# A fused attention and feed-forward kernel: third-weight loads moved ahead of a batch, and that batch's phases moved later among the weight products

## The chip, the cores and the metric

One Trainium2 chip, one core. The metric is device time in microseconds (us) from launch to end, as the median of several executions. The profile's "span" is the part of one execution from its first to its last instruction.

## What is computed

The reference is sparse attention with 8 batches, 8 heads, 576 tokens and 64 channels a head. Heads 0 to 3 look back over the last 31 tokens and themselves (local), heads 4 to 7 over tokens at multiples of 32 (strided). The attended values, as 4608 tokens of 512 channels, go through a multiplicative feed-forward layer:

```python
mask_local = (rel >= 0) & (rel < stride)
mask_strided = (rel >= 0) & (pos[None, :] % stride == pos[:, None] % stride)
...
attn = attn / (np.sum(attn, axis=-1, keepdims=True) + 1e-09)
return np.matmul(attn, v).astype(np.float32)
...
a = x @ w1
b = x @ w2
h = a * b @ w3
return (h @ w_out).astype(np.float32)
```

q, k and v are [8, 8, 576, 64], w1 and w2 [512, 1024], w3 [1024, 1024], w_out [1024, 512], all float32. The kernel works in float16 with float32 accumulation.

## The kernel before

**Folding.** Since nothing stands between the last two products, w3 @ w_out is computed once in the kernel (`w34`, [1024, 512]). w3 comes in 8 blocks of 128 rows (`load_w3`, L149). `fold_tr(jc)` (L528) transposes block jc on TensorE (PE), eight 128x128 transposes into one PSUM bank, then DVE copies one half of it into `w3T[0]` and ACT the other into `w3T[1]`. `fold_mm(jc)` (L537) multiplies by w_out in two halves of four products each, and DVE (even jc) or ACT (odd jc) copies the result to `w34`.

**Loads.** Every load is a DMA issued by SP, in the order in which the code calls it, into one of nine float32 staging buffers; a cast on GpSimd (POOL), in the same order, makes the float16 copy. For a batch: `load_qk(b, 0)` and `load_qk(b, 1)` bring the first 512 tokens of q and k for the local and the strided heads, `load_rest(b)` the last 64 tokens of all heads, `load_vL(b)` and `load_vS(b)` the values. A DMA also waits until the earlier transfer that used its semaphore, one of eight, has landed. The output writes, issued by ACT, use the same eight.

**Pairs.** The heads of a batch are worked in four pairs, two local and two strided; `pairs[4:8]` (p4 to p7) are batch 1, p8 is the first of batch 2. The first two batches go phase by phase: `ah_T` (L321) transposes q and k of a pair, `ah_R` (L343) the last 64 tokens of all pairs of the batch, `ah_S` (L395) makes the scores in two halves, with an exponential on ACT and a mask product on DVE (L403) for each, `ah_PV(s, g)` (L407) multiplies one half by the values and normalizes on DVE (`norm`, L422, two instructions, L426 and L427), `ph_T2` (L430) transposes the result into `xT` (ACT copies). From batch 2 on `ph_TS(s, t)` (L557) makes the scores of pair s and the transposes of pair t together, `ph_PV` (L300) the values product (PE at L317); `ph_TS(None, p8)` makes p8's transposes alone, the batch's last 64 tokens among them (PE at L232 and L240).

**Tiles.** The feed-forward part goes over 9 tiles of 512 tokens: `ab_parts(tch)` (L447) gives 32 steps of two products each, four steps for one block of 128 columns (a over channels 0 and 1, a over channels 2 and 3, b likewise), `o_parts(tch)` (L496) 16 steps of the output product, with an ACT copy and a DMA write to memory for every 128 tokens.

**PSUM.** Three pools: `psF` with three banks (fold, tiles, strided `ah_T`), `psB` with two buffers of two banks (scores, transposes of `ph_TS`, values products), `psM` with one bank (local `ah_T`, `ah_R`, `ph_T2`). A new tile waits until the one that held its buffer has been read.

**Order.** PE's order is the order of the code. The stretch that the change touches is written by hand: `units` holds the 23 fold steps and 8 pairs of output steps of tile 0, and `plan` says after which unit each phase of batch 1 is put:

```python
for jc in range(KF):
    h0, h1 = fold_mm(jc)
    units.append(h0)
    if jc + 1 < KF:
        units.append(lambda jc=jc: fold_tr(jc + 1))
    units.append(h1)
units += halves(o_parts(0))
```

After it, each tile's 48 steps fill the gaps of the list `stream`, which holds the later batches' phases with 48 marks (`GAP`) in a batch; `host(units, upto)` (L631) spreads units evenly over the marks up to `upto`. SP's and POOL's order is the order of the calls; ACT and DVE instructions are put in order by the scheduler of the language.

Of the kernel before, what the change touches and what calls it, by code (L numbers as in the profile page):

```python
# [19 lines left out]
def kernel(  # L20
# [49 lines left out]
    def pe(ins):  # L70
        return tc.keep_in_program_order(ins)

    def copy(eng, out, in_):
        if eng == "a":
            nc.scalar.copy(out=out, in_=in_)  # L75
        elif eng == "v":
            nc.vector.tensor_copy(out=out, in_=in_)  # L77
        else:
            nc.gpsimd.tensor_copy(out=out, in_=in_)  # L79
# [63 lines left out]
    def load_wo(g, eng):  # L143
        src = moe_w_out.rearrange("(c p) n -> p c n", p=P)
        st = stgp.tile([P, 2, DM], FP32, tag="stg")
        nc.sync.dma_start(st, src[:, 2 * g:2 * g + 2, :])
        copy(eng, woh[:, 2 * g:2 * g + 2, :], st)

    def load_w3(jc, eng):  # L149
        st = stgp.tile([P, DF], FP32, tag="stg")  # L150
        nc.sync.dma_start(st, moe_w3[bass.ds(jc * P, P), :])
        t = ffn.tile([P, DF], FP16, tag="w3n", bufs=6)
        w3n[jc] = t
        copy(eng, t, st)
# [13 lines left out]
    def load_qk(b, grp, engs="pp"):  # L168
        for nm, ten, eng in (("q", q, engs[0]), ("k", k, engs[1])):
            st = stgp.tile([P, 4, 4, D], FP32, tag="stg")  # L170
            nc.sync.dma_start(st.rearrange("p h c d -> p h (c d)"),  # L171
                              ten[b, 4 * grp:4 * grp + 4, 0:NM].rearrange("h (p c) d -> p h (c d)", c=4))
            t = qkp.tile([P, 4, 4, D], FP16, tag=f"{nm}{grp}")
            copy(eng, t, st.rearrange("p h c d -> p c h d"))
            x16[(b, nm, grp)] = t

    def load_rest(b, eng="p"):
        st = stgp.tile([P, H, D], FP32, tag="stg")
        for i, ten in enumerate((q, k)):
            nc.sync.dma_start(st[64 * i:64 * i + 64], ten[b, :, NM:S].rearrange("h p d -> p h d"))  # L180
        t = qkp.tile([P, H, D], FP16, tag="r")
        copy(eng, t, st)
        x16[(b, "r")] = t
# [246 lines left out]
    def ph_T2(s):  # L430
        w, n = s.w, s.n
        ps = psM.tile([P, 1024], FP16, tag="m")
        for t in range(n):
            pe(nc.tensor.transpose(ps[:, t * w:(t + 1) * w],  # L434
                                   s.xqs[0:w, t].rearrange("p h d -> p (h d)"),
                                   id16[0:w, 0:w]))
        o = xT[s.hp][:, S * s.b:S * s.b + S]
        if s.local:
            copy("a" if s.b < AHEAD else "v", o, ps[:, 0:S])
        else:  # L440
            nc.scalar.copy(out=o.rearrange("x (p c) -> x p c", c=n),  # L441
                           in_=ps[:, 0:S].rearrange("x (c p) -> x p c", p=w))
# [4 lines left out]
    def ab_parts(tch):  # L447
        tok = bass.ds(tch * NT, NT)
        res = []

        def first():
            abts[tch] = ffn.tile([P, KF, NT], FP16, tag="abt", bufs=4, name=f"abt{tch}")

        for jc in range(KF):
            st = {}

            def a(qt, jc=jc, st=st):
                if qt == 0:
                    if jc == 0:
                        first()  # L460
                    st["a"] = psF.tile([P, NT], FP32, tag="f", name="aps")
                for ci in (2 * qt, 2 * qt + 1):
                    pe(nc.tensor.matmul(st["a"], w1h[:, ci, bass.ds(jc * P, P)], xT[ci][:, tok],  # L463
                                        start=(ci == 0), stop=(ci == KM - 1)))
                if qt:
                    asb = ffn.tile([P, NT], FP32, tag="asb")
                    nc.scalar.copy(out=asb, in_=st["a"])  # L467
                    st["asb"] = asb

            def bb(qt, jc=jc, st=st):  # L470
                if qt == 0:
                    st["b"] = psF.tile([P, NT], FP32, tag="f", name="bps")
                for ci in (2 * qt, 2 * qt + 1):
                    pe(nc.tensor.matmul(st["b"], w2h[:, ci, bass.ds(jc * P, P)], xT[ci][:, tok],  # L474
                                        start=(ci == 0), stop=(ci == KM - 1)))
                if qt:
                    nc.vector.tensor_mul(abts[tch][:, jc, :], st["b"], st["asb"])  # L477

            res += [lambda f=f, qt=qt: f(qt) for f in (a, bb) for qt in range(2)]
        return res  # L480

    def acc_parts(lhs, rhs, done, n):
        st = {}
        m = KF // n

        def part(i):
            if i == 0:
                st["ps"] = psF.tile([P, NT], FP32, tag="f", name="ops")
            for ci in range(m * i, m * i + m):
                pe(nc.tensor.matmul(st["ps"], lhs(ci), rhs(ci), start=(ci == 0), stop=(ci == KF - 1)))  # L490
            if i == n - 1:
                done(st["ps"])

        return [lambda i=i: part(i) for i in range(n)]

    def o_parts(tch):  # L496
        res = []
        for ts in range(NT // P):
            def done(ps, ts=ts):
                osb = ffn.tile([P, DM], FP32, tag="osb", bufs=3)  # L500
                nc.scalar.copy(out=osb, in_=ps)  # L501
                nc.scalar.dma_start(out_r[tch * (NT // P) + ts], osb)

            if tch + 1 < NTILE or ts + 1 < NT // P:
                res += acc_parts(lambda ci, ts=ts: abts[tch][:, ci, bass.ds(ts * P, P)],
                                 lambda ci: w34[:, ci, :], done, 4)
        return res
# [38 lines left out]
    stream = []  # L546
    batch_end = {}
# [68 lines left out]
    for p, s in enumerate(pairs):  # L616
        b, i = divmod(p, 4)
# [11 lines left out]
    pos = [0]  # L629

    def host(units, upto):  # L631
        n = len(units)
        total = sum(x is GAP for x in stream[pos[0]:upto])
        done = 0
        for i, u in enumerate(units):
            tgt = total * i // n
            while pos[0] < upto and (stream[pos[0]] is not GAP or done < tgt):
                x = stream[pos[0]]
                pos[0] += 1
                if x is GAP:  # L640
                    done += 1
                else:
                    x()
            u()
        for x in stream[pos[0]:upto]:
            if x is not GAP:
                x()
        pos[0] = upto
# [9 lines left out]
    load_w3(0, "p")  # L658
    for g in range(4):
        load_wo(g, "p")  # L660
    load_w3(1, "p")
    load_w3(2, "p")
    load_qk(1, 0)
    load_w3(3, "p")
    load_rest(1)
    load_w3(4, "p")
    load_vL(1, (0,))
    load_w3(5, "p")
    load_w3(6, "p")
    load_vL(1, (1,))  # L670
    load_w3(7, "p")
    load_qk(1, 1)
    load_vS(1)

# [10 lines left out]
    units = []  # L685
# [4 lines that stand above are left out]
# [1 line left out]
        units.append(h1)  # L691
    units += halves(o_parts(0))
    p4, p5, p6, p7, p8 = pairs[4:9]
    plan = ((6, ah_T, p4), (9, ah_R, 1), (10, ah_T, p5), (11, ah_S, p4), (13, ah_S, p5),
            (14, ah_PV, p4, 0), (15, ah_PV, p4, 1), (18, ph_T2, p4), (20, ah_PV, p5, 0), (21, ah_PV, p5, 1),
            (21, ah_T, p6), (22, ah_T, p7), (23, ph_T2, p5), (23, ah_S, p6), (24, ah_S, p7),
            (26, ah_PV, p6, 0), (27, ah_PV, p6, 1), (27, ph_TS, None, p8), (28, ah_PV, p7, 0),
            (29, ph_T2, p6), (29, ah_PV, p7, 1), (31, ph_T2, p7))
    for i, u in enumerate(units, 1):
        u()  # L700
        if i == 23:
            load_qk(2, 1)
            load_vS(2)
        for x in plan:
            if x[0] == i:
                x[1](*x[2:])
    for tch in range(1, NTILE):
        units = ab_parts(tch) + o_parts(tch)
        if tch + 1 < B:
            more = tch + 2 < B  # L710
            if more:
                load_qk(tch + 2, 0)
                load_rest(tch + 2)
                load_vL(tch + 2)
            marks = [i for i in range(pos[0], batch_end[tch + 1]) if stream[i] is GAP]
            mid = marks[len(marks) // 2 - 1] + 1
            host(units[0:24], mid)
            if more:
                load_qk(tch + 2, 1)
                load_vS(tch + 2)  # L720
            host(units[24:], batch_end[tch + 1])
        else:
            for u in units:
                u()
# [31 lines left out]
```

## Time and profile before

| | |
|---|---|
| median of 3 runs | 279.38 us (278.61 to 280.46) |
| the profiled execution | 279.19 us |
| its span | 277.5 us |
| PE busy | 261.1 us (94%) |
| DVE, ACT, POOL busy | 145.7, 147.6, 116.1 us |
| read and written | 38.80 and 9.44 MB |

"Busy" counts the time in which an engine has at least one instruction at work. Matmuls overlap one another, so a step's cost on PE is the distance between the starts of its matmuls, not the sum of their durations. In a timeline row the columns are start, duration from the first start to the last end, engine, line, operation, output and inputs, count, and in brackets the idle time before it and who ended it. In a windows row they are the stretch, its length, then busy time and instructions of PE, PE's weight loads, DVE, ACT and POOL, the granted clock, the mean busy share of the 16 DMA engines (transfers that overlap can push it over 1) and GB/s.

### The profile page before, as it was taken

What the parts mean: (1) busy time and instruction counts of PE and PEld (TensorE: products, weight loads), DVE (VectorE), ACT (ScalarE), POOL (GpSimd) and SP (SyncE); (2) the same over time, 40 slices, a digit from 0 to 9 for tenths busy, and PEclk for the clock granted to TensorE, in tenths of its full rate; (3) what the DMA queues carried; (4) which work ended last, traced back from release to release, by engine and by line L of the source; (5) the groups of instructions that cost most, each with busy time, mean ns of one, the idle gap of its engine ahead of it and who ended that gap; (6) DMA issues with size and microseconds to landing.
All of it is one profiled execution on the core that took longest, in us unless ns stands there. A gap on an engine that the chain in (4) does not pass through costs nothing.

```text
span 277.5 us, 6652 instructions
## 1 busy us (share of the span) xinstructions
PE 261.1 (94%) x2656; PEld 138.2 (50%) x2656; DVE 145.7 (53%) x281; ACT 147.6 (53%) x298; POOL 116.1 (42%) x134
## 2 busy tenths in 40 slices
PE   1889998788999999999999999999999999999995
PEld 0465454454555555555555555555555555444442
DVE  2565341745477547655765567466547653320320
ACT  2663335657666566656556564656665654323322
POOL 4677774965856947785585644100000000000000
PEclk9999999999999999999999999999999999999999
DMA  7999999999899989997999680210031012003004
GB/s 208 274 333 391 393 324 258 287 212 147 258 300 223 259 246 266 235 258 192 261 267 240 183 224 4 98 56 2 0 117 40 0 40 113 0 2 151 0 4 151
DMA packets 56752, 48.68 MB, mean 175 GB/s; under 512 B 29200, under 2 KB 45840, under 8 KB 56720
## 3 DMA queue, kind: packets, MB, share of 16 engines
q1 hardware_dynamic: 51536, 38.87, 55.8%
q10 hardware_dynamic: 5184, 9.37, 9.1%
q8 instruction: 21, 0.34, 0.5%
q14 instruction: 11, 0.09, 0.1%
HBM read 38.80 MB, written 9.44 MB: 174 GB/s over the span
## 4 chain that ended last, share of the span: by engine, by line
PE 75%; DMA 14%; POOL 4%; SPq 3%; DVE 1%; issue 1%; ACT 1%; POOLq 0%; ACTq 0%
PE ops L490 21%; PE aps L463 21%; PE bps L474 20%; DMA st<-in_moe_w_dram 8%; DMA st<-in_v_dram 6%; PE sps L317 4%; PE ps L434 3%; POOL t L79 2%; PE pt L232 2%; PE sps L275 2%; PE pt L275 1%; POOL v16L L193 1%; SPq L191 1%; DVE ptm L403 1%; SPq L171 1%
## 5 line engine op out<-in xcount | busy, mean ns | idle before, releaser
L474 PE MATMUL bps<-xT,w2h 128*128 128x512 f16 x288 | 76.1, 379 | 0.0
L463 PE MATMUL aps<-xT,w1h 128*128 128x512 f16 x288 | 74.6, 380 | 0.5 <-ACT xT L441 0.5
L477 DVE TENSOR_TENSOR abt<-bps,asb 128x512 f16<-128x512 f32 x72 | 49.4, 687 | 43.3 <-PE bps L474 28.1
L467 ACT COPY asb<-aps 128x512 f32<-128x512 f32 x72 | 43.1, 599 | 46.3 <-PE aps L463 44.7
L490 PE MATMUL ops<-w,abt 128*128 128x512 f16 x280 | 66.8, 379 | 0.0
L79 POOL CAST t<-st 128x1024 f16<-128x1024 f32 (+1 forms) x46 | 45.7, 1004 | 24.4 <-DMA st<-in_k_dram 11.9
L463 PEld LDWEIGHTS <-w1h 128*128 128x128 f16 x288 | 26.4, 98 | 29.7
L474 PEld LDWEIGHTS <-w2h 128*128 128x128 f16 x288 | 26.3, 98 | 27.6 <-POOL w2h L79 0.8
L490 PEld LDWEIGHTS <-abt 128*128 128x128 f16 x280 | 25.3, 98 | 26.5
L193 POOL CAST v16L<-st 32x768 f16<-32x768 f32 (+1 forms) x32 | 27.7, 865 | 14.3 <-DMA st<-in_v_dram 7.9
L501 ACT COPY osb<-ops 128x512 f32<-128x512 f32 x35 | 20.6, 588 | 19.4 <-PE ops L490 19.4
L295 ACT ACTIVATE pte<-sps 128x960 f16<-128x960 f32 (+1 forms) x24 | 23.9, 995 | 10.8 <-PE sps L275 10.8
L427 DVE TENSOR_TENSOR xqs<-sps,rcp 96x768 f16<-96x768 f32 (+1 forms) x24 | 24.4, 1018 | 0.5
L204 POOL CAST v16S<-st 72x1024 f16<-72x1024 f32 x16 | 17.1, 1074 | 17.4 <-PE pm L317 9.9
L296 DVE TENSOR_TENSOR ptm<-pte,maskL 128x1152 f16<-128x1152 f16 x12 | 11.5, 961 | 22.7 <-ACT pte L295 22.7
L441 ACT COPY xT<-ps 128x576 f16<-128x576 f16 x16 | 10.2, 640 | 22.7 <-PE ps L434 22.7
L296 DVE TENSOR_TENSOR ptm<-pte,maskS 72x1152 f16<-72x1152 f16 x12 | 10.4, 864 | 20.2 <-ACT pte L295 20.2
L75 ACT COPY qT<-pt 128x256 f16<-128x256 f16 (+2 forms) x48 | 17.6, 409 | 3.6 <-DVE kT L77 2.9
L317 PEld LDWEIGHTS <-ptm 72*128 72x128 f16 (+1 forms) x336 | 13.1, 97 | 6.5 <-DVE ptm L296 2.0
L490 PE MATMUL ops<-woh,w3T 128*128 128x512 f16 x64 | 16.1, 379 | 0.0
L434 PEld LDWEIGHTS <-xqs 72*128 72x128 f16 (+1 forms) x224 | 12.1, 97 | 7.5 <-DVE xqs L427 0.8
L434 PE MATMUL ps<-id,xqs 72*128 72x72 f16 (+1 forms) x224 | 13.5, 200 | 0.3 <-DVE xqs L427 0.3
(93 smaller groups left out, 252.2 us busy)
## 6 DMA issues: line engine op xcount, KB each, us to landing
out_dram<-osb ACTq DMA_DIRECT2D x35, 256.0 KB, 2.0
st<-in_q_dram SPq DMA_DIRECT2D x16, 512.0 KB, 5.7
st<-in_k_dram SPq DMA_DIRECT2D x16, 512.0 KB, 4.7
st<-in_moe_w_dram SPq DMA_DIRECT2D x16, 512.0 KB, 10.6
st<-in_v_dram SPq DMA_DIRECT2D x32, 144.0 KB, 6.1
st<-in_v_dram SPq DMA_DIRECT2D x16, 256.0 KB, 7.8
st<-in_moe_w_out_dram SPq DMA_DIRECT2D x4, 512.0 KB
st<-in_q_dram SPq DMA_DIRECT2D x8, 128.0 KB, 7.8
```

Source lines behind the costliest of these rows:

```text
L79: nc.gpsimd.tensor_copy(out=out, in_=in_)
L193: nc.gpsimd.tensor_copy(out=vt[pr, hs, :, 0:D], in_=st[pr])
L295: nc.scalar.activation(out=pte[0:kr, lo:hi], in_=src, func=AF.Exp, bias=0.0, scale=scale)
L296: nc.vector.tensor_mul(ptm[0:kr, 0:2 * S].rearrange("p (a x) -> p a x", x=w), pte[0:kr].rearrange("p (a x) -> p a x", x=w), _ap(mk, 0, [[m ...
L317: pe(nc.tensor.matmul(xps[:, h, i * 65:i * 65 + 65], s.ptm[0:kr, c0:c0 + P], vt[0:kr, 2 * (s.hp % 2) + h, c, :], start=True, stop=True))
L427: nc.vector.tensor_mul(s.xqs[0:w, c0:c0 + l].rearrange("p i h d -> p h i d"), xv[:, :, :, 0:D], _ap(rcp, 0, [[rcp.ap[0][0], w], [ST, 2], [ ...
L434: pe(nc.tensor.transpose(ps[:, t * w:(t + 1) * w], s.xqs[0:w, t].rearrange("p h d -> p (h d)"), id16[0:w, 0:w]))
L463: pe(nc.tensor.matmul(st["a"], w1h[:, ci, bass.ds(jc * P, P)], xT[ci][:, tok], start=(ci == 0), stop=(ci == KM - 1)))
L467: nc.scalar.copy(out=asb, in_=st["a"])
L474: pe(nc.tensor.matmul(st["b"], w2h[:, ci, bass.ds(jc * P, P)], xT[ci][:, tok], start=(ci == 0), stop=(ci == KM - 1)))
L477: nc.vector.tensor_mul(abts[tch][:, jc, :], st["b"], st["asb"])
L490: pe(nc.tensor.matmul(st["ps"], lhs(ci), rhs(ci), start=(ci == 0), stop=(ci == KF - 1)))
```

## The change

Four parts:

1. **Loads.** w3 blocks 1 to 4 are loaded, and cast, ahead of batch 1's first q and k instead of blocks 1 and 2; blocks 5, 6 and 7 each move ahead by one or two places.
2. **Plan.** Batch 1's phases start after unit 10 instead of unit 6 and end after unit 31. The output transposes of p7 leave the plan.
3. **Tile 1.** Its first two steps are put after the scores of p8 and ahead of `ph_T2(p7)`, and four more behind it, in an order that takes the steps on channels 0 and 1 first; the six marks are skipped.
4. **Later tiles.** The place at which the second half of a batch's loads is called moves from behind the 24th mark to ahead of the 24th from the end, that is behind the next `ph_TS`. The units there are split from the end.

```diff
     for g in range(4):
         load_wo(g, "p")
-    load_w3(1, "p")
-    load_w3(2, "p")
+    for jc in range(1, 5):
+        load_w3(jc, "p")
     load_qk(1, 0)
-    load_w3(3, "p")
+    load_w3(5, "p")
     load_rest(1)
-    load_w3(4, "p")
+    load_w3(6, "p")
     load_vL(1, (0,))
-    load_w3(5, "p")
-    load_w3(6, "p")
+    load_w3(7, "p")
     load_vL(1, (1,))
-    load_w3(7, "p")
     load_qk(1, 1)
     load_vS(1)
...
-    plan = ((6, ah_T, p4), (9, ah_R, 1), (10, ah_T, p5), (11, ah_S, p4), (13, ah_S, p5),
-            (14, ah_PV, p4, 0), (15, ah_PV, p4, 1), (18, ph_T2, p4), (20, ah_PV, p5, 0), (21, ah_PV, p5, 1),
-            (21, ah_T, p6), (22, ah_T, p7), (23, ph_T2, p5), (23, ah_S, p6), (24, ah_S, p7),
-            (26, ah_PV, p6, 0), (27, ah_PV, p6, 1), (27, ph_TS, None, p8), (28, ah_PV, p7, 0),
-            (29, ph_T2, p6), (29, ah_PV, p7, 1), (31, ph_T2, p7))
+    plan = ((10, ah_T, p4), (13, ah_R, 1), (14, ah_T, p5), (15, ah_S, p4), (17, ah_S, p5),
+            (19, ah_PV, p4, 0), (20, ah_PV, p4, 1), (22, ph_T2, p4), (22, ah_PV, p5, 0), (23, ah_PV, p5, 1),
+            (24, ah_T, p6), (25, ph_T2, p5), (25, ah_T, p7), (26, ah_S, p6), (27, ah_S, p7),
+            (28, ah_PV, p6, 0), (29, ah_PV, p6, 1), (29, ph_TS, None, p8), (30, ah_PV, p7, 0),
+            (31, ph_T2, p6), (31, ah_PV, p7, 1))
...
+    tile1 = ab_parts(1) + o_parts(1)
+    stream[pos[0]]()
+    tile1[0]()
+    tile1[4]()
+    ph_T2(p7)
+    for i in (2, 1, 3, 5):
+        tile1[i]()
+    pos[0] += 7
     for tch in range(1, NTILE):
-        units = ab_parts(tch) + o_parts(tch)
+        units = tile1[6:] if tch == 1 else ab_parts(tch) + o_parts(tch)
...
-            mid = marks[len(marks) // 2 - 1] + 1
-            host(units[0:24], mid)
+            mid = marks[-24]
+            host(units[0:-24], mid)
...
-            host(units[24:], batch_end[tch + 1])
+            host(units[-24:], batch_end[tch + 1])
```

## Prediction

> **What bounds the kernel now.** I read the page's slices first. TensorE is full from slice 8 on, its clock is never throttled, and the DMA engines are full through the first half.
>
> ```profile
> PE   1889998788999999999999999999999999999995
> PEclk9999999999999999999999999999999999999999
> DMA  7999999999899989997999680210031012003004
> ```
>
> So time can be saved only where PE has holes, between slices 3 and 11. The windows narrow that to 40 to 70 us, where w3 is folded with w_out, tile 0's output is made, and batch 1's attention is put between:
>
> ```profile
> 40.00:45.00 5.00, 4.44 (x39) 2.58 (x38) 1.45 (x3) 2.17 (x5) 2.28 (x3) 1.00 1.25 214
> 50.00:55.00 5.00, 3.51 (x45) 2.00 (x44) 4.28 (x8) 2.75 (x5) 4.76 (x6) 1.00 1.04 309
> 65.00:70.00 5.00, 4.26 (x63) 2.52 (x62) 4.37 (x8) 2.74 (x6) 3.52 (x4) 1.00 0.73 139
> 70.00:75.00 5.00, 5.00 (x77) 3.09 (x76) 2.71 (x7) 2.77 (x7) 4.65 (x6) 1.00 0.80 257
> ```
>
> PE's waits from 37 to 78 us (total, times, longest) say for what: mostly casts on POOL, which themselves wait for loads.
>
> ```profile
> PE trp L532 <- POOL t L79: 2.0, 2, 1.5
> PE tps L331 <- POOL t L79: 1.0, 1, 1.0
> PE pt L232 <- DVE rcp L426: 0.5, 1, 0.5
> PE rps L353 <- POOL t L79: 0.5, 1, 0.5
> PE sps L373 <- ACT pte L402: 0.4, 2, 0.2
> ```
>
> PE's timeline gives the two ends of the stretch (first fold product, first P·V product of batch 2) and the places that decide below:
>
> ```profile
> 37.56 1.03 PE L490 MATMUL ops<-woh,w3T 128*128 128x512 f16 x4
> 52.37 0.62 PE L532 MATMUL trp<-id,t 128*128 128x128 f16 x8 [1.49 <-POOL t L79]
> 69.23 0.41 PE L232 MATMUL pt<-id,t 64*128 64x64 f16 x16 [0.51 <-DVE rcp L426]
> 69.46 0.30 PE L240 MATMUL pt<-id,t 64*128 64x64 f16 x8
> 71.99 0.42 PE L416 MATMUL xps<-v16S,ptm 72*128 72x65 f16 x8
> 77.53 0.53 PE L317 MATMUL sps<-v16L,ptm 128*128 128x65 f16 x12
> ```
>
> Both orders put the same 392 matmuls between the first and the last of these lines. By start-to-start distances, 108 products of 512 columns take 0.216 each (23.3), 92 transposes of 128 columns 5.7, 192 narrow ones 5.3: 34.3 us. The stretch takes 39.97, so 5.7 is waiting. After it the engine orders are the old ones, and PE has no holes: what is won or lost at 77.53 stays to the end.
>
> POOL's timeline shows which load each cast waited for: blocks 2 and 3 of w3, batch 1's remainder rows, and batch 2's.
>
> ```profile
> 37.65 1.04 POOL L79 CAST t<-st 128x1024 f16<-128x1024 f32 x1 [0.24 <-DMA st<-in_moe_w_dram]
> 42.83 1.04 POOL L79 CAST t<-st 128x1024 f16<-128x1024 f32 x1 [0.97 <-DMA st<-in_moe_w_dram]
> 45.25 0.61 POOL L79 CAST t<-st 128x512 f16<-128x512 f32 x1 [1.37 <-DMA st<-in_k_dram]
> 68.20 0.62 POOL L79 CAST t<-st 128x512 f16<-128x512 f32 x1 [0.26 <-DMA st<-in_k_dram]
> ```
>
> **What the change removes.** The loads of w3 blocks 3 and 4 (and, further on, 5 to 7) pass batch 1's on SP, and their casts pass on POOL, which sits waiting for loads here anyway. Blocks 1 and 2 are cast 1.29 apart (36.36, 37.65), so 3 and 4 are done at 40.0 and 41.3. The fold reaches their transposes at 42.8 and 45.4: the waits for w3 (2.0) go. Block 5 comes near 46.5, needed at 48.7; 6 and 7 likewise. Pairs 6 and 7 are transposed one to two output halves later, after their keys' cast (60.3): that 1.0 goes too.
>
> **What it adds**, walking the new order with the old durations. Batch 1's remainder rows now stand behind five w3 blocks instead of three: 45.25 plus 2 x 1.3 gives a cast at 47.9, done 48.5. PE has by then 9 fold halves (7.8), 4 block transposes (1.8) and pair 4's (0.45) behind it, 47.6: wait 0.9. Pair 5's transposes share one PSUM bank with the remainder's, whose four ACT copies free it 1.26 after (45.92 to 47.18 in the old order); only 0.68 of PE work lies between: 0.6. Block 6's copy on DVE stands behind pair 4's two mask products of about 1.0: scores at 51.1, copy done about 3.4 later, PE there after 2.9: 0.5. Scores of pair 7 behind two exponentials: 0.6, as now (64.36 to 64.70, 64.94 to 65.24). Pair 8's transposes and pair 7's first P·V wait for normalizations: 0.1 and 0.4.
>
> Then the end of the batch. Pair 7's last P·V is now directly followed by pair 8's scores, whose PSUM buffer it must give back. DVE shows the price:
>
> ```profile
> 72.45 0.20 DVE L426 RECIPROCAL rcp<-xps 72x8 f32<-72x8 f32 x1 [0.18 <-PE xps L416]
> 72.69 0.69 DVE L427 TENSOR_TENSOR xqs<-xps,rcp 72x512 f16<-72x512 f32 x1
> ```
>
> From 71.99 to 73.38 is 1.39, of which the P·V itself covers 0.24: wait 1.1, with all of PE queued behind it and, through the scores, ACT's exponentials. In the old order two output halves (1.73) lay there; if they covered it, it cost nothing. Last, tile 1's products over channels 2 and 3 wait for the output transposes' copy, which on ACT follows two exponentials and a copy (0.99, 0.34, 0.61): 0.4.
>
> Together 0.9 + 0.6 + 0.5 + 0.6 + 0.1 + 0.4 + 1.1 + 0.4 = 4.6 against 5.7: a gain of 1.1. But batch 2's remainder rows bound it. Their cast ends at 68.82 in either order, since the same bytes are loaded before. From there to the 77.53 event the new order has 6.1 of PE work and the waits 0.4 + 1.1 + 0.4: 8.0, so 76.8, a gain of 0.7. I take 0.8, between the two and nearer the bound. The walk over the old order, done the same way, lands within 0.15 of the trace at 69.23 and 77.53.
>
> **What is moved without a price.** The later tiles' loads of a batch's second half are written down after the next scores instead of before them: SP's sequence is unchanged. The first output write is issued near 63 instead of 67.73. Each load waits for the transfer that used its semaphore, one of eight, before it: SP shows batch 2's second key load at 73.03, when that write had landed (67.73 plus 5.2). Now the second query load stands behind the write, until about 68.2 (67.45 now), and the keys follow at 68.6; they are needed near 80 and cast by 75.
>
> **Against it: the write meets the loads.** The write of 256 KB now falls between 64 and 68, while batch 2's remainder rows come in. The windows have the DMA share at 0.67 (64 to 66) and 0.73 (66 to 68), so 1.2 us of idle engine time; the write needs 1.1 at the 246 GB/s of 60 to 62. Cost between 0 and 1.1; I take 0, as there is room, and keep 1.1. The Trainium skill (DMA: Bandwidth & Descriptors, Queues, rings and completion order) states that each engine takes turns between its queues packet by packet, so a write is served at once and not behind the loads. By that rule the rows come up to 1.1 later and the sum is 279.5.
>
> **The sum.** The profiled execution took 279.19, 277.5 of it span; that is 0.19 under the median of 279.38. 279.19 - 0.8 = 278.4.
>
> **Rivals.** First, slower: two output writes hold up batch 2's remainder rows. For: their issue moves to 63 and 66.5, before the cast at 68.2, and every later step hangs on it. Against: the idle share above. It decides from a delay of 0.8; at 1.1 to 2.2 for one or two writes the time is 279.5 to 280.6, middle 280.0.
>
> Second, also slower: DVE's mask products. Two rows of one shape:
>
> ```profile
> 51.60 1.02 DVE L403 TENSOR_TENSOR ptm<-pte,maskL 128x576 f16<-128x576 f16 x1 [0.19 <-ACT pte L402]
> 53.37 0.47 DVE L403 TENSOR_TENSOR ptm<-pte,maskL 128x576 f16<-128x576 f16 x1
> ```
>
> Of batch 1's eight, five take 0.9 to 1.27, with a POOL cast beside them, and three 0.45 to 0.47. With all eight at 1.0 the chain through scores and P·V is 1.5 longer: 279.9. The Trainium skill (SBUF — State Buffer, Who interferes with whom) says that a DVE instruction with two SBUF inputs and a POOL instruction that reads SBUF block each other; the trace agrees. The walk already has most of them long.
>
> Third, no effect: batch 1's remainder comes another 1.3 late (one block more), 0.4 of it hidden in the wait for batch 2's: 279.3.
>
> Fourth, more gain: pair 8's scores do not wait for the buffer (1.1) nor tile 1 for the copy (0.4): 276.9. Against: the built order has pair 8's scores waiting for DVE.
>
> **Numbers.** Chances: forecast 0.50 (277.8 to 279.0), writes 0.17, mask products 0.10, no effect 0.13, more gain 0.10. The range goes from 276.7 to 280.6, over the rivals' middles. A measurement of this kernel can tell about 1% (2.8 us) from no change. Below 276.6 lies a part of the fourth and what I have not seen, 0.09; above 282.2 only a collision worse than any above, 0.06; within, 0.85.
>
> **What would show it.** Right: no wait of L532 for POOL; 0.5 to 1.5 before L353; L240's first row at 68.6 to 69.2; about 1.1 before L275 with DVE as releaser; the first L317 at 76.5 to 77.0. Wrong: batch 2's remainder cast after 69 (writes), L353's wait over 2 (loads), or any hole after 80 us.

## The result, and the profile after

The changed kernel took 277.71 us (median of 12 runs, 276.79 to 281.82), the kernel before on the same chip 279.43 (12 runs, 278.27 to 281.88). The ratio is 0.9932, with a 95% interval from 0.9907 to 0.9958: about 1.9 us less, measurable but under one per cent. The forecast was 278.4. The profiled execution took 278.08, of which the span is 276.2. Medians here and below are over all runs; the ratios leave out runs more than 1.5% above the fastest of their kernel (281.48 and 281.82 here, two each in e3 and f4 below).

The page's slices, in the order shown for the kernel before (PE busy, granted clock, DMA share):

```profile
PE   1888999999899999999999999999999999999995
PEclk9999999999999999999999999999999999999999
DMA  7999999999899859897997860310031012003004
```

The holes of PE between slices 3 and 11 are nearly closed; the clock is as before. The windows of the same stretches (length, then busy time and instructions of PE, PE's weight loads, DVE, ACT and POOL, granted clock, DMA share, GB/s):

```profile
40.00:45.00 5.00, 5.00 (x37) 2.75 (x36) 1.75 (x5) 2.09 (x4) 3.47 (x4) 1.00 1.14 306
50.00:55.00 5.00, 5.00 (x56) 2.52 (x54) 3.54 (x5) 4.12 (x9) 4.12 (x6) 1.00 1.14 276
65.00:70.00 5.00, 4.50 (x69) 2.35 (x63) 4.84 (x9) 2.71 (x5) 4.30 (x6) 1.00 0.92 265
70.00:75.00 5.00, 4.13 (x64) 2.47 (x62) 3.04 (x8) 3.66 (x8) 4.81 (x7) 1.00 0.94 282
```

PE's busy time from 40 to 45 went from 4.44 to 5.00 and from 50 to 55 from 3.51 to 5.00; from 70 to 75 it fell from 5.00 to 4.13. So the gain is made early and a part of it is given back near 72. PE's waits from 37 to 78 us say what each is:

```profile
PE sps L275 <- DVE xqs L427: 0.9, 1, 0.9
PE tps L331 <- ACT kT L75: 0.4, 1, 0.4
PE xps L416 <- DVE ptm L403: 0.4, 1, 0.4
PE ops L490 <- DVE w3T L534: 0.2, 1, 0.2
PE aps L463 <- ACT xT L441: 0.2, 1, 0.2
```

Not one wait for POOL is left; before, POOL ended 3.5 us of PE's waits (2.0 at L532, 1.0 at L331, 0.5 at L353). All that is listed now is new: PSUM buffers and copies that come too late for the new order. PE's timeline has the two ends of the stretch and the places between that the prediction named:

```profile
38.25 1.03 PE L490 MATMUL ops<-woh,w3T 128*128 128x512 f16 x4
48.26 0.39 PE L353 MATMUL rps<-id,t 128*128 128x128 f16 x4
49.50 0.61 PE L331 MATMUL tps<-id,t 128*128 128x128 f16 x8 [0.41 <-ACT kT L75]
67.99 0.41 PE L232 MATMUL pt<-id,t 64*128 64x64 f16 x16
68.22 0.30 PE L240 MATMUL pt<-id,t 64*128 64x64 f16 x8
72.47 0.39 PE L275 MATMUL sps<-qT,kT 64*128 64x96 f16 x10 [0.87 <-DVE xqs L427]
75.16 0.38 PE L463 MATMUL aps<-xT,w1h 128*128 128x512 f16 x1 [0.15 <-ACT xT L441]
76.24 0.53 PE L317 MATMUL sps<-v16L,ptm 128*128 128x65 f16 x12
```

From the first fold product to batch 2's first P·V product it is now 76.24 - 38.25 = 37.99 us, before 39.97: 1.98 less. Up to L240 the difference is 1.93 (29.97 against 31.90), behind it 0.05 (8.02 against 8.07). This execution reached its first fold product 0.69 later than the one profiled before (38.25 against 37.56), though PE's order up to there is the same; over all the profiles below, that start lies anywhere between 37.45 and 38.80. It has nothing to do with the change, and it is why stretches are compared here and not times of day. From the first L317 to PE's last instruction it is 196.66 after and 196.62 before. So 0.69 - 1.98 + 0.04 = -1.25, the difference of the two spans (276.2 and 277.5) to a tenth, and what was won at L317 stayed to the end.

POOL's timeline: w3 block 4, batch 1's remainder, and one row for two casts, batch 2's first keys and its remainder.

```profile
40.61 1.04 POOL L79 CAST t<-st 128x1024 f16<-128x1024 f32 x1 [0.26 <-DMA st<-in_moe_w_dram]
...
47.18 0.61 POOL L79 CAST t<-st 128x512 f16<-128x512 f32 x1 [0.48 <-DMA st<-in_k_dram]
...
64.26 1.82 POOL L79 CAST t<-st 128x1024 f16<-128x1024 f32 x2 [0.85 <-ACT pte L402]
```

Batch 1's remainder is cast at 47.18 to 47.79, ahead of PE's arrival at 48.26. Batch 2's remainder is done at 64.26 + 1.82 = 66.08, where it was 68.82 before. Both differ from what was forecast, and both are followed up below.

### The profile page after: what moved, and what is told of

It is laid out like the page before. It is cut to its first block, busy times and chain, and to the rows that moved or that the text cites. A ratio compares the mean times of both kernels' runs of the same rounds, so it can differ in the third digit from the quotient of the medians.

```text
span 276.2 us, 6648 instructions
## 1 busy us (share of the span) xinstructions
PE 261.8 (95%) x2656; PEld 138.4 (50%) x2656; DVE 147.6 (53%) x281; ACT 147.8 (54%) x298; POOL 115.6 (42%) x134
## 3 DMA queue, kind: packets, MB, share of 16 engines
HBM read 38.80 MB, written 9.44 MB: 175 GB/s over the span
## 4 chain that ended last, share of the span: by engine, by line
PE 88%; DVE 5%; ACT 3%; DMA 2%; issue 1%; SPq 1%; DVEq 0%
PE ops L490 24%; PE aps L463 23%; PE bps L474 22%; PE sps L317 4%; PE ps L434 3%; DMA st<-in_k_dram 2%; DVE xqs L427 2%; PE sps L275 2%; DVE ptm L403 2%; PE pt L232 2%; PE xps L416 1%; PE pt L275 1%; PE tps L331 1%; PE trp L532 1%; ACT pte L402 1%
## 5 line engine op out<-in xcount | busy, mean ns | idle before, releaser
L296 DVE TENSOR_TENSOR ptm<-pte,maskS 72x1152 f16<-72x1152 f16 x12 | 11.7, 973 | 20.2 <-ACT pte L295 20.2
L317 PEld LDWEIGHTS <-ptm 72*128 72x128 f16 (+1 forms) x336 | 13.1, 97 | 6.5 <-DVE ptm L296 2.0
L434 PEld LDWEIGHTS <-xqs 72*128 72x128 f16 (+1 forms) x224 | 12.1, 97 | 7.5 <-DVE xqs L427 0.6
L434 PE MATMUL ps<-id,xqs 72*128 72x72 f16 (+1 forms) x224 | 13.5, 200 | 0.3 <-DVE xqs L427 0.3
```

Of the source, the lines that this page charges most:

```text
L296: nc.vector.tensor_mul(ptm[0:kr, 0:2 * S].rearrange("p (a x) -> p a x", x=w), pte[0:kr].rearrange("p (a x) -> p a x", x=w), _ap(mk, 0, [[m ...
L317: pe(nc.tensor.matmul(xps[:, h, i * 65:i * 65 + 65], s.ptm[0:kr, c0:c0 + P], vt[0:kr, 2 * (s.hp % 2) + h, c, :], start=True, stop=True))
L434: pe(nc.tensor.transpose(ps[:, t * w:(t + 1) * w], s.xqs[0:w, t].rearrange("p h d -> p (h d)"), id16[0:w, 0:w]))
```

## The experiments

All comparisons are with runs of the kernel before on the same chip, taken in turn with it. "Stretch" is, in each kernel's one profile, the time from the first fold product to batch 2's first P·V product at L317; "POOL waits" are those of PE's listed waits in it that POOL ends. "Ahead" counts the w3 blocks that are loaded ahead of batch 1's first q and k, from block 1 on. Each ratio is to the kernel before as it ran beside that kernel: its medians were 279.43 for "after", 278.99 for e1 to e4, 279.14 for f1 to f4 and 279.20 for g1 to g3. So across letters the ratios are compared, not the times.

| kernel | ahead | plan | POOL waits | stretch | median, us | ratio to before (95%) |
|---|---|---|---|---|---|---|
| before | 2 | old | 3.5 | 39.97 | 279.43 | |
| e1 | 4 | old | 3.2 | 39.83 | 279.45 | 1.0009 (0.9982 to 1.0036) |
| e2 | 2 | new | 1.8 | 40.82 | 280.81 | 1.0068 (1.0041 to 1.0094) |
| f2 | 3 | new | 1.7 | 39.37 | 279.51 | 1.0010 (0.9986 to 1.0034) |
| after | 4 | new | 0 | 37.99 | 277.71 | 0.9932 (0.9907 to 0.9958) |
| f1, the same | 4 | new | 0 | 37.66 | 277.56 | 0.9927 (0.9901 to 0.9953) |
| f3 | 5 | new | 1.5 | 39.14 | 278.72 | 0.9979 (0.9958 to 0.9999) |
| g3 | 5, remainder earlier | new | 0.9 | 38.73 | 278.23 | 0.9967 (0.9939 to 0.9995) |
| e3 | 4 | new, tile 1 old | 0 | 37.24 | 277.05 | 0.9931 (0.9906 to 0.9955) |
| e4 | 4 | new, tile 1 covers | 0.3 | 37.06 | 276.97 | 0.9918 (0.9894 to 0.9942) |
| f4 | 4 | new, tile 1 covers | 0.4 | 37.88 | 277.67 | 0.9932 (0.9905 to 0.9959) |
| g1, ten buffers | 2 | old | 2.9 | 39.02 | 279.36 | 1.0002 (0.9985 to 1.0020) |
| g2, eight buffers | 4 | new | 0 | 37.45 | 277.27 | 0.9941 (0.9917 to 0.9965) |

### The loads alone (e1)

The kernel before with the changed load order, its plan and tile 1 as they were:

```diff
-    load_w3(1, "p")
-    load_w3(2, "p")
+    for jc in range(1, 5):
+        load_w3(jc, "p")
     load_qk(1, 0)
-    load_w3(3, "p")
+    load_w3(5, "p")
     load_rest(1)
...
```

> Only the order of the loads is changed; plan and tile 1 are the old ones. Theory (the two parts pay only together): batch 1's query and key casts come 2.6 us later while its first transposes stay at unit 6, so the 2.0 us of waits of the block transposes for POOL go, but pair 4's transposes wait 1.4 for the queries and 1.4 for the keys and the remainder's 1.4: slower than before by 0.5 to 1.5 us (ratio 1.002 to 1.005). Rival (earlier w3 is the gain by itself): faster than before by 1 to 2 us (0.993 to 0.997).

PE's waits from 37 to 78 us in its profile:

```profile
PE tps L331 <- POOL t L79: 2.0, 2, 1.1
PE rps L353 <- POOL t L79: 0.9, 1, 0.9
PE sps L373 <- ACT pte L402: 0.4, 2, 0.2
PE xps L416 <- POOL v16L L79: 0.3, 1, 0.3
```

The wait of L532 for w3 is gone, as the prediction says. In its place PE waits for what the blocks overtook: the q and k of pair 4 (L331), batch 1's remainder (L353), its values (L416), together 3.2 where it was 3.5. The time is unchanged: the waits came mostly where the theory put them, but smaller than the 4.2 it gave, and neither its slower time nor the rival's faster one was measured. A load that passes another one does not remove a wait, it hands it on, unless the work that needs the overtaken load is also put later.

### The plan and tile 1 alone (e2)

The changed kernel with the old load order:

```diff
-    for jc in range(1, 5):
-        load_w3(jc, "p")
+    load_w3(1, "p")
+    load_w3(2, "p")
     load_qk(1, 0)
-    load_w3(5, "p")
+    load_w3(3, "p")
...
```

> The new plan and the new tile 1 with the old order of loads. Theory (together only): the fold runs ahead of its w3 blocks, which come behind batch 1's rows; the block transposes wait for POOL 1.6, 1.0 and 1.9 us: slower than before by 1 to 2.5 us (1.004 to 1.009). Rival (the later plan alone is the gain, the same bytes arrive at the same time in any order): as the changed kernel, 0.993.

It is 0.7% slower than before. The start of its list of PE's waits:

```profile
PE trp L532 <- POOL t L79: 1.8, 1, 1.8
PE trp L532 <- ACT kT L75: 1.1, 1, 1.1
PE sps L275 <- DVE xqs L427: 0.9, 1, 0.9
```

The later plan has its own waits (L275) and runs into the late w3 block all the same. Loads alone give nothing, the plan alone loses 0.7% (280.81 against 278.99 of before beside it), both together win 0.7%: the gain is not in either part.

### How far ahead (f2, f3, g3), and the same kernel again (f1)

```diff
# f2: three blocks ahead
+    load_w3(1, "p"); load_w3(2, "p"); load_w3(3, "p")
     load_qk(1, 0)
+    load_w3(4, "p")
     load_rest(1)
+    load_w3(5, "p")
     load_vL(1, (0,))
+    load_w3(6, "p")
     load_vL(1, (1,))
+    load_w3(7, "p")
# f3: five ahead, then qk, 6, rest, 7, vL, vL
# g3: five ahead, then qk, rest, 6, vL, 7, vL
```

> The changed kernel once more, unaltered, for a second profile of it. Two theories of why batch 2's remainder rows were cast by 66.1 in it and by 68.8 in the kernel before. Order: the load order together with the plan brings them, so this profile has the cast done at 65.5 to 67.0 again, no wait of PE for POOL between 37 and 78 us, and the stretch from the first fold product to batch 2's first P.V product (the stretch, below) at 37.7 to 38.3. Chance: the loads of one execution differ from those of the next, so the cast may be done anywhere from 66 to 69; a cast after 67.8 speaks for this, with the stretch 0.5 to 1.5 longer. Time by either 276.5 to 278.0, ratio to the kernel before 0.991 to 0.996.

> The changed kernel with w3 blocks 1 to 3 ahead of batch 1's first q and k, and 4 to 7 after each of the next loads in turn (instead of 1 to 4 ahead). By when casts arrive alone: block 4 is cast at about 45.4, PE's transposes of it come at about 45.7, so nothing is waited for there, batch 1's remainder comes 1.3 earlier, and the time is that of the changed kernel within 0.3 us (277.0 to 277.9). If grouping w3's loads makes all loads faster, batch 2's remainder is done later, at 67 to 68.5, between 66.1 (four ahead) and 69.8 (two ahead with the same plan), PE waits for it 0.3 to 1.5 ahead of L240, and the time is 0.5 to 1.5 us over the changed kernel's (277.9 to 279.2).

> The changed kernel with w3 blocks 1 to 5 ahead of batch 1's first q and k. By when casts arrive: pair 4's q and k are cast 1.3 later, by 46.2, PE wants them at 45.7 (wait 0.5, PE for POOL at L331), the remainder rows by 49.1 against 48.8 (0.3 at L353), so the time is 0.8 above the changed kernel's: 278.2 to 278.8. If grouping makes all loads faster, the same waits stand, but batch 2's remainder is done by 65 to 66; as nothing waits for it at 66.1 already, that gains nothing, and the time is again 278.2 to 278.8; a cast later than 66.5 speaks against this theory.

> Five w3 blocks ahead of batch 1's first q and k as in f3, but batch 1's remainder rows ahead of block 6. If the 1.5 us that PE waited in f3 for the remainder is all that made five worse than four, this wait goes to 0 to 0.3, block 6 (cast by 50.0, as in the changed kernel) is waited for by at most 0.2, and the time is that of the changed kernel: 277.0 to 277.9, a stretch of 37.4 to 38.0. If five blocks ahead cost something of themselves (q and k of pair 4 later, POOL behind), the stretch stays above 38.5 and the time above 278.2.

The changed kernel repeated itself (277.56; stretch 37.66, no POOL wait). Three ahead and five ahead are both slower than the changed kernel beside them on the same chip (279.51 and 278.72 against 277.56; g3 278.23 against 277.27 of g2, though the ratios' intervals of these two overlap), and their timelines show why. First f2, then f3, then g3, the PE rows that POOL ends:

```profile
53.20 0.62 PE L532 MATMUL trp<-id,t 128*128 128x128 f16 x8 [0.47 <-POOL t L79]
57.40 0.62 PE L532 MATMUL trp<-id,t 128*128 128x128 f16 x8 [1.20 <-POOL t L79]
```

```profile
49.56 0.40 PE L353 MATMUL rps<-id,t 128*128 128x128 f16 x4 [1.45 <-POOL t L79]
```

```profile
46.35 0.40 PE L331 MATMUL tps<-id,t 128*128 128x128 f16 x4 [0.91 <-POOL t L79]
```

With three ahead, blocks 6 and 7 come late (block 7 is then loaded behind batch 1's second values, and POOL works on those from 53.21 to 56.03). With five, PE waits 1.5 for batch 1's remainder (0.3 had been expected there and 0.5 at L331, where none came; the time was as expected). With five and the remainder put ahead of block 6, that wait goes, as expected, but the keys of pair 4 are cast later (45.25 to 46.29) and PE waits for them. Neither of the two readings given for f2 was right in full: the waits were neither "none" nor at L240. In g3 the second reading (that five ahead costs something of itself) held.

Read down the table, the stretches of the changed plan go with the POOL waits: 37.45 to 37.99 with none (after, f1, g2), 38.73 with 0.9, 39.14 with 1.5, 39.37 with 1.7. Take these waits off, and from e2's 40.82 its 1.8 and the 1.1 for ACT, and 37.4 to 38.0 is left in all seven that have the changed kernel's tile 1. The same for the old plan gives 36.5 (before), 36.6 (e1), 36.1 (g1). So the change is two things of opposite sign: 3.5 us of waits for POOL go, and the new plan with its tile 1 costs about 1.5 of its own; 39.97 - 3.5 + 1.5 = 38.0. The 1.5 is what the subtraction leaves, not a measured wait; the listed waits that POOL does not end rose from 0.9 to 2.1, which accounts for 1.2 of it. With the other orders of tile 1 that follow, 37.2 (e3), 36.8 (e4) and 37.5 (f4) is left, so a part of it belongs to tile 1 and not to the plan.

### Tile 1's first steps (e3, e4, f4)

e3 takes part 3 and part 4 of the change back (tile 1 and the later tiles in the old order, p7's output transposes in the plan again); e4 and f4 move tile 1's steps ahead of pair 8's scores, so as to cover the 0.9 at L275:

```diff
# e3
-            (31, ph_T2, p6), (31, ah_PV, p7, 1))
+            (31, ph_T2, p6), (31, ah_PV, p7, 1), (31, ph_T2, p7))
...
-    stream[pos[0]]()
-    tile1[0]()
-    tile1[4]()
-    ph_T2(p7)
...
# e4
+    tile1[0]()
+    tile1[4]()
+    ph_T2(p7)
     stream[pos[0]]()
# f4
+    tile1[0]()
+    tile1[4]()
     stream[pos[0]]()
     ph_T2(p7)
```

> New loads and new plan; tile 1 in the old order, with the output transposes of pair 7 behind unit 31 and ahead of pair 8's scores. Theory (the new tile 1 moves one wait, 1.1 us ahead of pair 8's scores, and adds 0.4 for the copy; the old order waits about 0.8 ahead of the transposes and nothing behind): equal to the changed kernel or up to 0.5 us faster than it (0.991 to 0.994 of before). Rival (the new order of tile 1 is part of the gain): 0.5 to 1 us slower than the changed kernel (0.995 to 0.997).

> The changed kernel with tile 1's first two steps and then pair 7's output transposes put ahead of pair 8's scores, instead of behind them. Theory (PE's wait of 0.9 ahead of pair 8's scores is for pair 7's normalization and nothing else, and what PE saves there stays to the end): two steps of 0.43 lie in that wait, so the wait shrinks to about 0.1 and the time is 0.6 to 1.0 us under the changed kernel (0.989 to 0.991 of before). Rival (a load of batch 2 or the exponentials bound the stretch, so that the wait only moves): the same as the changed kernel, 0.993.

> The changed kernel with tile 1's first two steps ahead of pair 8's scores instead of behind them (p7's output transposes stay behind the scores). The wait of 0.9 at L275 for pair 7's normalization is covered by 0.87 of PE work: the wait of L275 falls to 0 to 0.2. If that wait sets the end, the time falls by 0.5 to 0.9 against the changed kernel of the same call; if the exponentials and mask products of pair 8, whose scores start no earlier, set the next P.V product, a wait of the same size comes at L317 (0.5 to 0.9) and the time stays within 0.3.

e3 has no wait at L275; its list has 0.4 and 0.3 at L434, where p7's transposes now wait. Its stretch is 0.2 to 0.75 shorter than those of the changed kernel, f1 and g2, but its ratio is that of the changed kernel (0.9931), so parts 3 and 4 bring nothing that the time shows. f4 and e4 each lose the wait of L275 and find it again one step on. From f4's timeline, then e4's list from 66 to 100 us:

```profile
71.68 0.39 PE L275 MATMUL sps<-qT,kT 64*128 64x96 f16 x10
...
74.38 0.38 PE L463 MATMUL aps<-xT,w1h 128*128 128x512 f16 x1 [1.02 <-ACT xT L441]
```

```profile
PE sps L317 <- DVE ptm L296: 1.2, 2, 0.7
PE pt L240 <- POOL t L79: 0.3, 1, 0.3
```

In f4 the two steps fill the 0.9, and the scores come hardly sooner for it (4.07 after L240, 4.25 in the changed kernel); tile 1's products over channels 2 and 3 then wait 1.0 for `xT`, which comes through p7's normalization, transposes and an ACT copy. The stretch is 37.88, with 0.4 of waiting for POOL in it, and the ratio is that of the changed kernel. The place of the new wait was not the one expected (L317). e4 puts the transposes early as well, has the shortest stretch (37.06), and then waits 1.2 at L317 for mask products, 0.7 of it behind the stretch. Its time, 276.97, is the lowest of all; with the overlap of the intervals its ratio cannot be told from the changed kernel's. So the 0.9 is only the front of a longer chain, from pair 7's P·V through its normalization and transposes to tile 1 and pair 8's exponentials.

### Staging buffers (g1, g2)

Batch 2's remainder rows were cast by 68.8 in the kernel before and by 66.1 after, against the forecast. One candidate was that SP holds loads back until POOL has emptied a staging buffer:

```diff
# g1, on the kernel before
-    stgp = ctx.enter_context(tc.tile_pool(name="stgp", bufs=9))
+    stgp = ctx.enter_context(tc.tile_pool(name="stgp", bufs=10))
-        t = ffn.tile([P, DF], FP16, tag="w3n", bufs=6)
+        t = ffn.tile([P, DF], FP16, tag="w3n", bufs=4)
# g2, on the changed kernel
-    stgp = ctx.enter_context(tc.tile_pool(name="stgp", bufs=9))
+    stgp = ctx.enter_context(tc.tile_pool(name="stgp", bufs=8))
```

> The kernel before with ten float32 staging buffers instead of nine (paid for with four instead of six float16 buffers for w3). Two theories of why batch 2's remainder rows come at 68.8 in it and at 66.1 to 67.6 with four w3 blocks ahead. Staging: SP holds loads back until POOL has emptied a buffer (8.6 us of such waits between 40 and 66 us in the old order), so one buffer more cuts these waits to under 6 us and brings the remainder's cast to 67.0 to 68.0. Rate: the DMA engines are never short of issued loads there and only the mix of rows counts, so the cast is done at 68.4 to 69.2 as before. The time stays within 0.4 us of the kernel before by either, since PE's waits for w3 blocks and pairs 6 and 7 come earlier.

> The changed kernel with eight staging buffers instead of nine. Staging theory: SP's waits for POOL grow from 6 to over 8 us, batch 2's remainder is done at 67.8 to 69, PE waits for it 0.3 to 1.3 at L232 or L240, the time is 0.4 to 1.3 over the changed kernel's (278.0 to 278.9). Rate theory: done at 66.0 to 67.6, time within 0.4 of the changed kernel's.

POOL's row for batch 2's first keys and remainder, in g1 and then in g2:

```profile
65.86 1.82 POOL L79 CAST t<-st 128x1024 f16<-128x1024 f32 x2 [1.54 <-DMA st<-in_k_dram]
```

```profile
64.38 2.03 POOL L79 CAST t<-st 128x1024 f16<-128x1024 f32 x2 [0.52 <-DMA st<-in_k_dram]
```

With one buffer fewer the casts of the changed kernel are done at 66.41, SP's waits for POOL between 40 and 66 us do not grow (5.3 in all), PE does not wait, and no time is lost (277.27): buffers do not set it. With one more, the old order has the casts done at 67.68, inside that theory's 67.0 to 68.0, but not by its way: SP still waits 6.5 for POOL there (2.6 at L171, 1.8 at L191, 1.5 at L151, 0.6 at L180), and the 2.5 that is gone stood at batch 2's values, which are issued behind these rows. The rate theory's 68.4 to 69.2 was missed too. The time of g1 is that of before, as both had it.

So what remains is a list. End of batch 2's remainder cast with the old loads: 68.82, 69.81 (e2), 67.68 (g1). With three ahead 67.79, with five 66.46 (f3) and 67.69 (g3). With four ahead and the new plan 66.08, 66.36 (f1), 66.40 (e3), 66.41 (g2), 67.4 (e4), 67.55 (f4); with four ahead and the old plan 68.2 (e1). The spread within one load order and plan is 1.5 (counted from the start of w3 block 1's cast in the same profile, 29.3 to 31.2), so one profile's arrival is not a fixed point; the difference between the orders is larger than that only in company with the plan. Why the loads get on faster is not settled.

## Why the prediction came out as it did

The total lay within the range given, and the mechanism (w3 waits go, the plan pays some back near L275) is shown by e1, e2 and the waits. The size was off: 0.8 was forecast, and 1.9 was measured by the ratio (1.7 by the medians of all runs), 1.98 in the profiled stretch. 277.71 lies between the forecast (278.4) and the middle of the fourth rival, more gain (276.9), and 0.1 below the forecast's own range of 277.8 to 279.0.

**Right.** PE's wait at L532 for POOL (2.0) and at L331 for pairs 6 and 7 (1.0) went. L275 waits 0.87 with DVE's normalization as releaser (1.1 forecast). From L240 to L317 it is 8.02 (8.0 forecast), though made up otherwise: PE is idle for 1.1 instead of the 1.9 of waits, and busy for 6.9 instead of 6.1. The first L317 came at 76.24, or at 75.55 counted from the old execution's first fold product; 76.5 to 77.0 had been given, so it was earlier than that. The writes were issued at 62.20 and 65.77 (near 63 and 66.5 forecast), batch 2's second keys at 66.35 instead of 73.03, and no hole came after 80 us. L240's row at 68.22 is below the 68.6 to 69.2 that was given.

**Wrong: the bound.** The step "their cast ends at 68.82 in either order, since the same bytes are loaded before" failed. With the changed order it ended at 66.08, and PE arrived at L232 at 67.99 without a wait. The old order had shown no wait for these rows to begin with: at 69.23 L232 waited for DVE (`rcp`), and L240 followed at 69.46, 0.6 after the cast. In ten of the eleven experiment profiles PE did not wait for these rows at L232 or L240 either; in e4 it waited 0.3. So there was no bound at 76.8, and taking 0.8 instead of the walk's 1.1 was a step in the wrong direction.

**Mis-sized: the terms of the walk.** Forecast against the profile after:

| term | forecast | measured |
|---|---|---|
| L353, batch 1's remainder | 0.9 | 0 |
| pair 5's transposes, `psM` | 0.6 | 0.4 |
| block 6's fold half, behind mask products | 0.5 | 0 |
| pair 7's scores, behind exponentials | 0.6 | 0 |
| pair 8's transposes | 0.1 | 0 |
| pair 7's first P·V | 0.4 | 0 |
| pair 8's scores, L275 | 1.1 | 0.9 |
| tile 1 for `xT` | 0.4 | 0.2 |
| not forecast: block 7's fold half, pair 6's first P·V | | 0.2 + 0.4 |
| sum | 4.6 | 2.1 |

The first missed by most. PE was where it was forecast (10.01 after the first fold product, 10.04 forecast), but the rows were cast earlier: I had added two w3 blocks at 1.3 each, 2.6, to the old 45.25, and the cast began at 47.18, only 1.9 later. In f4 it began 9.9 after the fold product instead of 8.9 and PE waited 0.4; in e1, 0.9; in f3, 1.5. So this term is real and lies just at its threshold in the changed kernel.

The listed waits fell from 4.4 to 2.1, by 2.3, and the stretch by 1.98. The windows of the two whole stretches, before and then after, show that the lists leave nothing out:

```profile
37.56:77.53 39.97, 35.57 (x394) 20.52 (x393) 20.63 (x41) 23.50 (x47) 26.96 (x30) 1.00 1.04 241
```

```profile
38.25:76.24 37.99, 35.87 (x393) 20.41 (x392) 21.90 (x42) 23.77 (x47) 30.13 (x32) 1.00 1.05 264
```

PE is idle for 39.97 - 35.57 = 4.40 and for 37.99 - 35.87 = 2.12, as listed. So the step "34.3 us. The stretch takes 39.97, so 5.7 is waiting" was wrong by 1.3: PE was busy for 35.57, more than its start-to-start distances add up to, and in the new order for 35.87. The forecast set its named new waits (4.6) against these 5.7. Against the 4.4 that PE did wait, its own terms say no gain. So two errors worked against each other (new waits sized 2.5 too large, old waiting 1.3 too large), and that the total fell in the range owes something to this luck.

Some smaller readings were loose, and nothing hangs on them. The 0.6 "as now" of pair 7's scores was 0.4 in the old list. PE's slices are full from the eleventh on, not from the eighth. The bounds beside the chances (276.6 and 282.2) are not those of the range (276.7 to 280.6); 277.71 lies inside both.

**The rivals.** Writes against loads: the first write was issued at 62.20, beside batch 2's remainder, and had landed by 65.87, when SP issued the load that waited for it; the rows were cast by 66.08, earlier than before, so the 0.8 to 1.1 was not paid. The Trainium skill (DMA: Bandwidth & Descriptors, Queues, rings and completion order) says that an engine serves its queues in turn, so the write is not put behind the loads. Its landing at most 3.7 us after the issue, while the loads issued beside it took 5.7 (median), agrees with that; the delay of the loads that was drawn from it does not show. Mask products: the eight take 6.8 together (1.64 for two, 0.95, 0.67, 2.56 for three, 0.94), not the 8 that the rival supposed, and only one wait of 0.4 hangs on them. The Trainium skill's statement that the two engines block each other (SBUF — State Buffer, Who interferes with whom) agrees with them: the seven that start while POOL casts or copies take 0.67 to 1.33 each, and the one at 66.37, while POOL is idle (66.08 to 66.59), takes 0.45. In the old order the eight take 6.6. No effect: it supposed another 1.3 of lateness for batch 1's remainder. That is about what f3 built (these rows are cast from 48.88, 1.7 later than in the changed kernel), and there PE does wait 1.5 and the time is 278.72. More gain: it needed L275 not to wait; L275 did wait, and the gain came from L353, block 6 and pair 7 instead. f4 has no wait at L275 and the ratio of the changed kernel, so covering that wait alone won nothing.

## What to carry to other kernels

Move a load and the work that needs the overtaken load together: each alone was worth nothing or lost 0.7%, both gave 0.7%, and one block more or less in the load order cost 0.4 to 0.8%. Before a wait is counted as removed by cover, follow the chain behind it to the next thing that needs the same producer; here the 0.9 at the scores came back as 1.0 at the products over `xT`. Compare listed waits with listed waits, and count an arrival time read off a single execution as uncertain (by 1.5 us here), not as a bound. Take waiting from PE's idle time, not from the stretch less its start-to-start distances; here that counted 1.3 us of busy time as waiting.

## What was not expected of the hardware

The DMA share did not tell how many bytes moved. Answers of the DMA view, from 62 to 66 us, of the kernel before and then of the changed kernel, with their queues (packets, MB, share of the 16 engines; q1 carries the loads, q10 the output writes):

```profile
DMA packets 1545, 0.56 MB, mean 139 GB/s; under 512 B 1337, under 2 KB 1544, under 8 KB 1544
...
q1 hardware_dynamic: 1544, 0.54, 95.8%
```

```profile
DMA packets 2666, 0.92 MB, mean 230 GB/s; under 512 B 2500, under 2 KB 2538, under 8 KB 2666
...
q1 hardware_dynamic: 2522, 0.66, 84.1%
q10 hardware_dynamic: 144, 0.26, 20.7%
```

The mean share is 0.98 and 1.05, yet one moved 1.65 times as much. Most of the difference is the first output write, which falls into this window only after the change: 0.26 of the 0.36 MB, in packets of 1.8 KB on average, for a share of 0.21. The loads alone differ too, though less: 0.54 MB at 0.96 and 0.66 MB at 0.84, so for the same share the changed kernel's loads moved 1.4 times as much, and in smaller packets (262 bytes on average against 350). Why is open. From 34 to 38 us, while weights came (405 of 458 packets of 2 KB and more), the changed kernel moved 407 GB/s at a share of 1.02. The Trainium skill (DMA: Bandwidth & Descriptors, Specifications) puts full rate at transfers of 512 bytes and up; that agrees with 407 against 139 and 230, where 87% and 94% of the packets are smaller, but it does not explain why the loads of the two kernels differ. In the kernel before, the share falls to 0.39 from 65 to 66 us while the keys, which POOL casts at 66.90, are still on their way; which engines they hang on was not looked into.
